# A state kept as diagonal blocks, and a turn of the queries moved behind the second of seven products

## The chip, the cores and the metric

The kernel runs on one core of one Trainium2 chip. Its time is the device time in microseconds (us) of one execution. PE is the matrix engine (PEld its weight loads), DVE the vector engine, ACT the scalar engine, POOL the GpSimd engine and SP the engine whose queue issues the DMAs. Every engine works through its own instructions in the order in which the program lists them, and waits at the first one whose inputs or buffers are not ready.

## The reference

Everything is float32. An RWKV-6 attention block of 4 batches, 8 heads, 768 tokens and a head width of 48 feeds a feed-forward block over 3072 tokens (width 384, inner width 2048):

```python
for t in range(S):
    cur = einsum('bhd,bhe->bhde', u * k[t], v[t])
    y[t] = einsum('bhd,bhde->bhe', r[t], state + cur)
    state = w[t][..., None] * state + einsum('bhd,bhe->bhde', k[t], v[t])
x = y.transpose(0, 2, 1, 3).reshape(B * S, H * D)
h = x @ w_in
out = (h * sigmoid(h)) @ w_out
```

The state of one head is a 48 x 48 matrix. The decay w[t] multiplies its rows.

## The kernel before

**Units.** The work is cut into 12 units, numbered 0 to 11. A unit is 128 tokens of two batches, with all eight heads. Heads stand in pairs on the partitions: the even head of a pair on partitions 0 to 47, the odd one on 64 to 111. In each unit the scan over 128 tokens is done in levels: queries (`tr`) and keys (`tk`) are multiplied by growing products of the decays (`tw`, `tw1` to `tw7`), and for each level PE multiplies keys by queries into scores. `y_state` multiplies the queries by the state, `y_values` the scores by the values, and `update` carries the state over to the next 128 tokens.

**The feed-forward part** of a unit follows one and two units later. `up` (8 steps, L1001) computes `h` and its silu `gt`; then seven products of half matrices, as in a Strassen-Winograd scheme, replace the eight of the plain second multiplication. `quarter(i, which)` (L1053) makes product number `which` of unit i: 16 matmuls of 128 x 192 (L1067) into a tile `p_o`, which has two buffers, and then the additions that use it. They are called q0 to q6 here. q0 is copied by ACT into `partial` (L1074); q1, q2, q3, q5 and q6 are each followed by one addition on DVE (L1076), q4 by two. A product can begin only when the addition of the product two before it has read its buffer. The inputs of three of the seven are differences that `sums` (L1049) makes on DVE.

**The order of the work** is written out by hand. For units 3 to 11 the loop at L1166 takes the lists ("groups") of steps that `mix(i)` returns, and after each group some of the steps of `downs(i - 2) + ups(i - 1)`: these are the seven products of the unit two before, and the eight `up` steps of the unit before. From unit 4 on the numbers of such steps after the groups are `(2, 1, 2, 2, 1, 1, 1, 2, 1, 1, 1)`: q0 and q1 stand behind the first group, q2 behind the second, q3 and q4 behind the third, q5 and q6 behind the fourth. When unit i is spoken of below, its seven products are those issued while `mix(i)` runs, so they belong to the output of unit i - 2.

The steps that the change and the profile below touch:

- `turn(i, b, name)` (L360) transposes the raw rows of one batch with one DVE instruction (L374). "Both" turns are two.
- `grow_own(i, l)` (L649) multiplies keys on POOL, two instructions (L654), and then calls `grow_queries(i, l)`, which multiplies the queries by the decays on DVE in place (L627).
- `start(i)` in `mix` gives the products of the decays for levels 1 to 6 on POOL (L422), and `grow_own(i, 1)`.
- `block_bonus(i, step)` (L505) multiplies parts of r, k and w on POOL (L507) for the scores inside a block of eight tokens. Steps 0 to 3 of a unit are done at the end of the unit before. Step 4 is two instructions that write the tile `ruk`, step 5 is four, and 6 and 7 are one each.
- `block_sum(i, step)` (L539) adds these up on DVE (L541): sum 0 reads the `ruk` of steps 0 and 1, sum 1 what step 2 left in `spare`, sum 2 the `ruk` of step 4 (four instructions). So step 4 on POOL has to wait until sum 0 has read the tile that it overwrites.
- `prepare(i, 3)` and `burst(i, 3)` make the queries of level 3 and the first score matmuls (L704), behind the seven products.
- `move_x(i - 1)` (L921) moves the result y into the layout of the feed-forward part with ten DMAs on SP's queue.
- `update(i, b)` (L885) multiplies the state by the last product of the decays on POOL (L898), and then adds keys times values from PSUM on DVE (L907). For the first 128 tokens it copies instead (L909).

The state of a head pair is kept in a row of 2 x 64 columns: the even head's matrix in columns 0 to 47 of its partitions, the odd head's in columns 64 to 111 of its own. The rest of the row is cleared once (`clear_state`, L403) and never used by a matmul.

Of the kernel before, what the change touches and what calls it, by code (L numbers as in the profile page):

```python
# [8 lines left out]
F32 = mybir.dt.float32  # L9
# [29 lines left out]
def kernel(  # L39
# [11 lines left out]
    nc = tc.nc  # L51

    B, H, S, D = r.shape
    DM, DF = moe_w_in.shape
    L = 128
    NL = 7
    NB = 2
    NP = H // 2
    PD = 64
# [14 lines left out]
    const = ctx.enter_context(tc.tile_pool(name="const", bufs=1))  # L74
# [9 lines left out]
    def bank(name, *dims):  # L84

        have = banks[name][turns_of[name] % 2][:]
        turns_of[name] += 1
        steps, n = [], 1
        for d in dims[::-1]:
            steps.insert(0, [n, d])  # L90
            n *= d
        return bass.AP(tensor=have.tensor, offset=have.offset, ap=[have.ap[0], *steps])
# [193 lines left out]
    make_identity(nc, ident)  # L286


    state = const.tile([128, B, NP, 2 * PD], F32, name="state")

    room = pt.tile([128, 4, DM // 2], F32, name="partial", bufs=1).rearrange("p x d -> p (x d)")
    spread = room[:, 0:4 * L].rearrange("p (s b t) -> p s b t", s=2, b=NB)
# [65 lines left out]
    tw, tr, tk, diag, kq, xt = {}, {}, {}, {}, {}, {}  # L358
# [473 lines left out]
    def values(i, b):  # L832
        return vq[i] if b == 1 else vt[i]

    def y_state(i):

        n, b0 = units[i]
        for e in range(2):
            p_yt[i, e] = bank("p_m", NP, L)
        for p in range(NP):  # L840
            for b in range(NB):
                for e in range(2):
                    rows = slice(PD * e, PD * e + D)
                    nc.tensor.matmul(y_place(i, e, p, b), lhsT=state[rows, b0 + b, p, rows],  # L844
                                     rhs=tr[i][rows, b * NP + p, :], start=(p < 2 and b == 0), stop=False)

        half = L // 2
        for p in range(NP):
            for b in range(NB):
                rows, at = slice(b * half, (b + 1) * half), (2 * p + b) * D  # L850
                nc.tensor.matmul(y_place(i, b, p, b)[:, 0:half], lhsT=whole[i][b][rows, at:at + D],
                                 rhs=score[rows, i % NSC, b, b * NP + p, 0:half], start=False, stop=False)

    def y_place(i, e, p, b):

        x = p % 2
        return p_yt[i, e][PD * x:PD * x + D, p // 2 * NB + b, :]
# [27 lines left out]
    def update(i, b):  # L885
        n, b0 = units[i]
        if n == S // L - 1:
            return
        if b == 0:
            p_kv[i] = bank("p_m" if i < NTOK else "p_sc", NB, NP, D)  # L890
        for p in range(NP):
            for e in range(2):
                nc.tensor.matmul(p_kv[i][PD * e:PD * e + D, b, p, :], lhsT=kq[i, b][:, p, PD * e:PD * e + D],
                                 rhs=values(i, b)[:, 2 * p + e, :], start=(b == 0 and p == 0),
                                 stop=(b == NB - 1 and p == NP - 1))
        new = state[:, b0 + b]
        if n > 0:
            nc.gpsimd.tensor_tensor(out=new, in0=new,  # L898
                                    in1=tw[i][NL][:, b * NP:(b + 1) * NP, :].to_broadcast([128, NP, 2 * PD]),
                                    op=ALU.mult)  # L900
        if b < NB - 1:
            return
        for e in range(2):
            rows, cols = slice(PD * e, PD * e + D), slice(PD * e, PD * e + D)
            new = state[rows, b0:b0 + NB, :, cols]
            if n > 0:
                nc.vector.tensor_tensor(out=new, in0=p_kv[i][rows], in1=new, op=ALU.add)  # L907
            else:
                (nc.scalar.copy if i == 0 else nc.vector.tensor_copy)(out=new, in_=p_kv[i][rows])  # L909
# [23 lines left out]
    def both(fn, i, *args):  # L933
        return [(fn, i, b, *args) for b in range(NB)]

    def block_loads(i, names="wkr"):
        return [(load_blocks, i, name, g) for name in names for g in range(4)]

    def mix(i):

        ahead = i + 1 < len(units)

        def at(now, *steps):
            return steps if now else ()

        def bonus_steps(j, *steps):
            return [(block_bonus, j, x) for x in steps]

        def sum_steps(j, *steps):
            return [(block_sum, j, x) for x in steps]  # L950

        def turns(j):
            return [*both(turn, j, "w"), (product, j, 0), *both(turn, j, "k")]

        def start(j):
            return [*[(product, j, l) for l in range(1, NL)], (grow_own, j, 1)]

        end = [[*at(ahead, *bonus_steps(i + 1, 0, 1, 2, 3))],
               [*at(i < len(units) - NB, (turn_apart, i), (turn_k, i)), (y_state, i), *both(y_values, i), *at(ahead, *turns(i + 1)),
                (sums, i - 1, FH // 2 - 2), *both(update, i), *at(not ahead, (move_x, i))]]  # L960
        if i < NPAIR:
            groups = [[*both(turn, i, "w"), (product, i, 0)],
                      [*both(turn, i, "k"), *both(turn, i, "r"), (odd_ones, i)], [(start_levels, i), (prepare_keys, i, 1)],
                      [(prepare, i, 1), *[(product, i, l) for l in range(1, NL)]],
                      [(burst, i, 1), (keep_level, i, 1)],
                      [(keep_level, i, 2), (go_on, i, 2)],
                      [(prepare, i, 3), (reverse_v, i), (bonus, i, 0)],
                      [(burst, i, 3), (keep_level, i, 3), (bonus_sum, i, 0), (bonus, i, 1), (bonus, i, 2)],
                      [(keep_level, i, 4), (go_on, i, 4), (bonus_sum, i, 1), (load_rk, i + 1), (load_u,)],
                      [(prepare, i, 5), (make_block_mask,), (bonus_spread, i), (bonus_write, i)],  # L970
                      [(burst, i, 5), (keep_level, i, 5), (keep_level, i, 6), (go_on, i, 6)], *end]
        else:
            groups = [[*both(turn, i, "r"), (grow_own, i, 0)], [*start(i), *sum_steps(i, 0, 1), *bonus_steps(i, 4, 5), (move_x, i - 1)],
                      [(odd_keys, i, 2), (grow_keys, i, 2, False), (grow_queries, i, 2), *sum_steps(i, 2)],
                      [(prepare, i, 3), *bonus_steps(i, 6, 7)],
                      [(burst, i, 3), (keep_level, i, 3), *sum_steps(i, 3, 4), (block_move, i), *at(ahead, (load_rk, i + 1))],
                      [(keep_level, i, 4), (go_on, i, 4)],
                      [(prepare, i, 5), (reverse_v, i)],
                      [(block_spread, i), (block_write, i)],
                      [(burst, i, 5), (keep_level, i, 5), (keep_level, i, 6), (go_on, i, 6)], *end]  # L980

        loads = [*at(i >= NPAIR and ahead, *block_loads(i + 1, "r")), *at(i + NSLOT < len(units), *block_loads(i + NSLOT, "wk"))]
        if i + 1 < len(units):
            loads.insert(len(loads) // 2, (load_values, i + 1))

        behind = groups[10 if i < NPAIR else 5 if i == NPAIR else 2:][:4 if i + NSLOT >= len(units) else None]
        for at, group in enumerate(behind):
            group += loads[at * len(loads) // len(behind):(at + 1) * len(loads) // len(behind)]
        return groups
# [127 lines left out]
    for l in range(1, NL):  # L1117
# [9 lines left out]


    others = {1: [(bonus_sum, 1, 0), (bonus_sum, 1, 1), (load_rk, 2), *blocks[8:12]], 2: [*both(update, 0)],
              3: [(bonus_spread, 1), (reverse_v, 1), (clear, 1), (load_values, 2)]}  # L1130

# [4 lines left out]
    for m in range(1, 4):  # L1136
# [4 lines left out]
    do((scores, 1, NL - 1), (bonus, 2, 0), (bonus, 2, 1), (join_weight, 8), (add_weight,), (bonus_sum, 2, 0), (bonus, 2, 2), (up, 0, 7), *both(y, 1), (turn_apart, 1),  # L1141
       (tail_weight, 9), (turn_k, 1), (dense_x, 1, 0), (head_weight, 9, [0]), (dense_x, 1, 1), (head_weight, 9, [1]),
       (join_weight, 9), (add_weight,), (tail_weight, 10), (head_weight, 10), *both(update, 1), (bonus_sum, 2, 1), (load_rk, 3), (up, 1, 0), *both(turn, 2, "w"))
    blocks = block_loads(3)

# [5 lines left out]
    for m in range(6):  # L1151
# [8 lines left out]
    do((burst, 2, 5), (keep_level, 2, 5), (keep_level, 2, 6), (go_on, 2, 6), (bonus_write, 2), (up, 1, 6), (weight_sums, 1),  # L1160
       (load_values, 3), (turn_apart, 2), (turn_k, 2), (up, 1, 7), (weight_sums, 2), (sums, 1, 2))
    do((sums, 1, 3), (y_state, 2), *both(y_values, 2), *both(update, 2),
       (move_x, 2),
       *blocks[7:])

    for i in range(3, len(units)):  # L1166
        steps = downs(i - 2) + ups(i - 1)
        groups = mix(i)
# [40 lines left out]
```

## Time and profile before

| what | value |
|---|---|
| median of 3 runs | 601.27 us (600.91 to 601.62) |
| the profiled execution | 601.18 us, with a span of 599.4 us from first to last instruction |
| granted clock of the matrix engine | 0.999 |
| POOL state multiplication L898 | 16 instructions, 1215 to 2079 ns, median 1266 |
| DVE state addition L907 | 16 instructions, median 551 ns |
| DVE transposes of r, L374 | 20 instructions, median 674 ns |
| DVE additions L1076 | 77 instructions, about 0.35 us each |

The profile comes from the one profiled execution. In its listings a row of a timeline has the start and the length in us, the engine, the line of the kernel, the operation, what it writes and reads with shapes, and how many instructions were merged. In brackets stand the idle time of the engine before it and what ended that idle time. A row of waits has the total, the number and the longest. Matmul ends are modelled, so a PE that is listed as busy is not always at its peak; a stall shows more surely as a later start of the next product.

### The profile page before, as it was taken

To read this page: it belongs to the slowest core of one execution; us is meant where nothing else is said; L and a number is where in the kernel's file an instruction comes from. 1 tells how busy PE (TensorE), PEld (TensorE's weight loads), DVE (VectorE), ACT (ScalarE), POOL (GpSimd) and SP (SyncE) were. 2 spreads that over 40 slices of the span, in tenths; PEclk is the share of its full clock that TensorE was granted. 3 is DMA by queue.
4 is the path that set the end of the run, shared out by engine and by line. 5 is a ranking of instruction groups with operands and counts; after the bars stand their busy time and mean duration, and the time that the engine had idled before them with its cause. 6 is when DMAs were issued, how large, how long until landed. Compare 5 with 4: busy or idle time off the path is not lost.

```text
span 599.4 us, 15465 instructions
## 1 busy us (share of the span) xinstructions
PE 590.6 (99%) x6142; PEld 529.7 (88%) x6142; DVE 417.5 (70%) x709; ACT 232.8 (39%) x516; POOL 361.3 (60%) x414
## 2 busy tenths in 40 slices
PE   8999999999999999999999999999999999999997
PEld 7787876799899899899899889889889889889997
DVE  7879788798696695696696696687588587542041
ACT  6788884431530530540350351361351251250110
POOL 6998778357678568278578478577567567500000
PEclk9999999999999999999999999999999999999999
DMA  9966794342542543642643643643543531101000
GB/s 225 306 143 176 165 277 49 54 80 48 129 61 62 108 68 54 134 63 52 137 63 54 134 61 53 135 61 53 112 77 52 121 57 27 36 2 28 27 1 26
DMA packets 203080, 53.45 MB, mean 89 GB/s; under 512 B 186752, under 2 KB 194816, under 8 KB 203008
## 3 DMA queue, kind: packets, MB, share of 16 engines
q1 hardware_dynamic: 201424, 51.88, 42.3%
q8 instruction: 48, 0.79, 0.6%
q10 hardware_dynamic: 1584, 0.59, 0.5%
q14 instruction: 24, 0.20, 0.1%
HBM read 43.21 MB, written 5.24 MB: 81 GB/s over the span
## 4 chain that ended last, share of the span: by engine, by line
PE 74%; DVE 9%; POOL 4%; DMA 4%; ACT 3%; issue 3%; SPq 3%; DVEq 0%; POOLq 0%; ACTq 0%
PE p_h L1001 31%; PE p_o L1067 31%; PE p_m L1023 3%; PE p_sc L704 2%; PE p_m L865 2%; DVE temps L1049 2%; SPq L123 1%; PE p_m L844 1%; PE p_m L704 1%; DVE score L722 1%; POOL w_in_sb L255 1%; DMA tokens_w<-in_w_dram 1%; POOL tk L645 1%; DVE p_w L242 1%; DMA raw<-in_r_dram 1%
## 5 line engine op out<-in xcount | busy, mean ns | idle before, releaser
L1001 PE MATMUL p_h<-xt,w_in_sb 128*128 128x256 f32 x1152 | 259.5, 382 | 0.8 <-POOL tk L669 0.7
L1001 PEld LDWEIGHTS p_h<-xt,w_in_sb 128*128 128x128 f32 x1152 | 215.6, 190 | 32.1 <-POOL tk L669 0.9
L1010 ACT ACTIVATE gt<-p_h 128x512 f32<-128x512 f32 x90 | 53.5, 596 | 175.4 <-PE p_h L1001 175.1
L645 POOL TENSOR_TENSOR tk<-tk,tw 128x256 f32<-128x256 f32 x128 | 94.6, 759 | 32.9 <-issue 20.8
L1067 PE MATMUL p_o<-own,temps 128*128 128x192 f32 x528 | 88.7, 327 | 0.7 <-DVE temps L1076 0.7
L1067 PEld LDWEIGHTS p_o<-own,temps 128*128 128x128 f32 x528 | 86.0, 190 | 1.6 <-DVE temps L1076 1.6
L507 POOL TENSOR_TENSOR ruk<-tokens_rk 128x768 f32<-128x768 f32 (+1 forms) x32 | 50.6, 1594 | 60.8 <-DMA tokens_rk<-in_k_dram 36.9
L1067 PE MATMUL p_o<-w_out_sb,gt 128*128 128x192 f32 x508 | 86.6, 327 | 0.0
L1067 PEld LDWEIGHTS p_o<-w_out_sb,gt 128*128 128x128 f32 x508 | 83.3, 190 | 1.0 <-DVE partial L1076 0.4
L1049 DVE TENSOR_TENSOR temps<-gt 128x256 f32<-128x256 f32 x84 | 54.9, 653 | 25.5 <-ACT gt L1010 25.3
L627 DVE TENSOR_TENSOR tr<-tr,tw 128x512 f32<-128x512 f32 x61 | 54.8, 899 | 18.3 <-PE p_m L704 14.6
L422 POOL TENSOR_TENSOR tw<-tw 128x256 f32<-128x256 f32 (+6 forms) x83 | 41.0, 494 | 35.8 <-DVE tw L374 31.9
L615 ACT COPY tk<-tk 128x256 f32<-128x256 f32 x52 | 21.0, 403 | 105.2 <-POOL tk L645 77.6
L1049 DVE TENSOR_TENSOR temps<-temps,gt 128x256 f32<-128x256 f32 x43 | 32.6, 759 | 1.5
L722 DVE COPY_PREDICATED score<-mask,p_sc 128x512 f32<-128x512 int8 x42 | 31.2, 799 | 3.5 <-PE p_sc L704 3.3
L1067 PE MATMUL p_o<-w_out_sb,temps 128*128 128x192 f32 x176 | 30.4, 326 | 0.0
L541 DVE TENSOR_REDUCE block_sums<-ruk 128x4 f32<-128x192 f32 (+1 forms) x48 | 24.2, 546 | 7.1 <-POOL ruk L507 7.1
L1067 PEld LDWEIGHTS p_o<-w_out_sb,temps 128*128 128x128 f32 x176 | 28.9, 190 | 0.0
L1076 DVE TENSOR_TENSOR partial<-p_o,partial 128x192 f32<-128x192 f32 x33 | 11.7, 354 | 24.6 <-PE p_o L1067 24.6
L1076 DVE TENSOR_TENSOR temps<-p_o,partial 128x192 f32<-128x192 f32 x22 | 7.9, 358 | 29.8 <-PE p_o L1067 23.5
L870 ACT COPY yt<-p_m 48x512 f32<-48x512 f32 x40 | 23.2, 580 | 13.8 <-PE p_m L865 13.1
L704 PEld LDWEIGHTS p_sc<-tr,tk 48*32 48x32 f32 (+1 forms) x1312 | 18.2, 119 | 11.1 <-issue 8.1
(188 smaller groups left out, 821.9 us busy)
## 6 DMA issues: line engine op xcount, KB each, us to landing
w_out_sb<-in_moe_w_in_dram SPq DMA_DIRECT2D x6, 768.0 KB, 7.5
w_out_sb<-in_moe_w_out_dram SPq DMA_DIRECT2D x4, 768.0 KB, 5.6
own<-in_moe_w_out_dram SPq DMA_DIRECT2D x4, 768.0 KB, 6.4
tokens_rk<-in_r_dram SPq DMA_DIRECT2D x8, 384.0 KB, 4.5
tokens_rk<-in_k_dram SPq DMA_DIRECT2D x8, 384.0 KB, 5.5
tokens_w<-in_w_dram SPq DMA_DIRECT2D x8, 384.0 KB, 6.6
xt<-yt SPq DMA_DIRECT2D x60, 48.0 KB, 2.0
raw<-in_w_dram SPq DMA_DIRECT2D x80, 32.0 KB, 2.0
```

The costliest lines, as they stand in the source:

```text
L422: engine.tensor_tensor(out=up, in0=t[:, :, 0::2], in1=t[:, :, 1::2], op=ALU.mult)
L507: mul = lambda out, one, two: nc.gpsimd.tensor_tensor(out=out, in0=one, in1=two, op=ALU.mult)
L541: add = lambda out, have: nc.vector.tensor_reduce(out=out, in_=have, axis=mybir.AxisListType.X, op=ALU.add)
L627: nc.vector.tensor_tensor(out=odd, in0=odd, in1=tw[i][l][:, :, 0::2][:, :, :, None].to_broadcast([128, Q, L >> (l + 1), c]), op=ALU.mult)
L645: nc.gpsimd.tensor_tensor(out=out, in0=have, in1=odd_products(i, l, b, *blocks), op=ALU.mult)
L704: nc.tensor.matmul(to, lhsT=tk[i][rows, X[l % 2] + p, x * m:(x + 1) * m], rhs=have, start=True, stop=True)
L722: nc.vector.copy_predicated(out=dst, mask=masks[l][:, :, None].to_broadcast([128, NB, NP, ni, c]), data=sc[e].rearrange("p (b q) (i c) -> ...
L870: nc.scalar.copy(out=yt[i][PD * e:PD * e + D, x::2, :, :], in_=p_yt[i, e][PD * x:PD * x + D].rearrange("p (q b) t -> p q b t", b=NB))
L1001: nc.tensor.matmul(p_h[:, a, :], lhsT=w_in_sb[:, c, f * 128:(f + 1) * 128], rhs=xt[i][:, c, :], start=(c == 0), stop=(c == KC - 1))
L1010: nc.scalar.activation(out=gt[i, m], in_=p_h, func=AF.Silu)
L1049: nc.vector.tensor_tensor(out=out, in0=one, in1=two, op=op)
L1067: nc.tensor.matmul(p, lhsT=left(f), rhs=right[:, f, :], start=(f == 0), stop=(f == FH - 1))
```

## The change

The state keeps only the 48 columns that are used: `[128, B, NP, 48]` instead of `[128, B, NP, 128]`. Both heads of a pair then have their matrix in columns 0 to 47, each on its own partitions. `y_state` and `update` address it accordingly, and the POOL multiplication of a batch has 4 x 48 elements to a partition instead of 4 x 128.

In `mix`, for units 4 to 11 (the branch that the diff shows; unit 3 has a list of its own), the first group becomes empty. The turns of r and `grow_own(i, 0)`, which stood ahead of q0 and q1, go to the head of the second group, ahead of `start(i)`. Block sum 1 and block bonus 5 go from the second group to the head of the third, that is behind q2. In the built program PE, ACT, POOL and SP have their instructions in the same order as before. On DVE the addition of q1 now stands ahead of the two turns and the first query step, and the addition of q2 ahead of block sum 1.

```diff
-    state = const.tile([128, B, NP, 2 * PD], F32, name="state")
+    state = const.tile([128, B, NP, D], F32, name="state")
...
-                    nc.tensor.matmul(y_place(i, e, p, b), lhsT=state[rows, b0 + b, p, rows],
+                    nc.tensor.matmul(y_place(i, e, p, b), lhsT=state[rows, b0 + b, p, :],
...
-                                    in1=tw[i][NL][:, b * NP:(b + 1) * NP, :].to_broadcast([128, NP, 2 * PD]),
+                                    in1=tw[i][NL][:, b * NP:(b + 1) * NP, :].to_broadcast([128, NP, D]),
...
-            rows, cols = slice(PD * e, PD * e + D), slice(PD * e, PD * e + D)
-            new = state[rows, b0:b0 + NB, :, cols]
+            rows = slice(PD * e, PD * e + D)
+            new = state[rows, b0:b0 + NB]
...
-            groups = [[*both(turn, i, "r"), (grow_own, i, 0)], [*start(i), *sum_steps(i, 0, 1), *bonus_steps(i, 4, 5), (move_x, i - 1)],
-                      [(odd_keys, i, 2), (grow_keys, i, 2, False), (grow_queries, i, 2), *sum_steps(i, 2)],
+            groups = [[], [*both(turn, i, "r"), (grow_own, i, 0), *start(i), *sum_steps(i, 0), *bonus_steps(i, 4), (move_x, i - 1)],
+                      [*sum_steps(i, 1), *bonus_steps(i, 5), (odd_keys, i, 2), (grow_keys, i, 2, False), (grow_queries, i, 2), *sum_steps(i, 2)],
```

## The prediction

> **What bounds the kernel now.** I read the page's busy times and slices first, then a table of busy time by unit, then the waits of PE, then the timeline of one undisturbed unit.
>
> ```profile
> PE 590.6 (99%) x6142; PEld 529.7 (88%) x6142; DVE 417.5 (70%) x709; ACT 232.8 (39%) x516; POOL 361.3 (60%) x414
> PE   8999999999999999999999999999999999999997
> ```
>
> TensorE is busy from end to end, so a change can win only PE's few stalls, or add some. By unit (start of one unit's seven products to the next; columns: stretch, length, PE busy, ...):
>
> ```profile
> 172.16:219.00 46.84, 46.53 (x498) 42.39 (x497) 35.56 (x59) 15.33 (x38) 33.45 (x38) 1.00 0.42 78
> 219.00:265.00 46.00, 46.00 (x498) 42.37 (x497) 33.38 (x55) 15.34 (x38) 28.71 (x35) 1.00 0.46 83
> 265.00:311.60 46.60, 46.43 (x498) 42.29 (x497) 35.32 (x59) 15.33 (x38) 32.59 (x37) 1.00 0.46 83
> ```
>
> Units 5 and 7 to 9 take exactly 46.00 us: no stall. Units 4 and 6 lose 0.6 to 0.8 us. The waits of the weight loads (total us, times, longest) say where:
>
> ```profile
> PEld p_o L1067 <- DVE temps L1076: 1.6, 3, 0.6
> PEld p_o L1067 <- DVE partial L1076: 0.4, 2, 0.2
> ```
>
> The products q0 to q6 have two PSUM buffers: q3 needs DVE's addition of q1, q5 that of q3. Unit 4, the bad case:
>
> ```profile
> 180.02 0.36 DVE L1076 TENSOR_TENSOR temps<-p_o,partial 128x192 f32<-128x192 f32 x1
> 180.44 5.47 PE L1067 MATMUL p_o<-own,temps 128*128 128x192 f32 x32 [0.31 <-DVE temps L1076]
> ```
>
> q3 could have started 7.80 after q0 (172.16), at 179.96; it starts 0.48 late, 0.41 after the addition began, and the restart costs 0.11 more (5.47 for a stretch of 5.36). Then q5 is held too: addition 185.42, start 185.82. Together 0.77 (19.06 from q0 to the next score matmuls, against 18.29 in unit 8); the same reading gives 0.63 in unit 6 and 0.57 in unit 3. **1.96 us of stall**, all because q1's addition is queued on DVE behind the turns of r. Now unit 8, undisturbed, DVE, POOL and PE:
>
> ```profile
> 360.95 1.29 DVE L374 STREAM_TRANSPOSE tr<-raw 128x512 f32<-128x512 f32 x2
> 362.27 1.05 DVE L627 TENSOR_TENSOR tr<-tr,tw 128x512 f32<-128x512 f32 x1
> 363.36 0.36 DVE L1076 TENSOR_TENSOR temps<-p_o,partial 128x192 f32<-128x192 f32 x1
> 363.63 0.68 DVE L627 TENSOR_TENSOR tr<-tr,tw 128x512 f32<-128x512 f32 x1
> 364.23 0.95 DVE L541 TENSOR_REDUCE block_sums<-ruk 128x16 f32<-128x768 f32 x1
> ...
> 367.71 1.13 DVE L541 TENSOR_REDUCE block_sums<-ruk 128x4 f32<-128x192 f32 x4 [0.89 <-POOL ruk L507]
> 368.76 0.35 DVE L1076 TENSOR_TENSOR partial<-p_o,partial 128x192 f32<-128x192 f32 x1
> ```
>
> ```profile
> 361.34 1.44 POOL L654 TENSOR_TENSOR tk<-tk,tw 128x256 f32<-128x256 f32 x2
> 365.26 2.42 POOL L507 TENSOR_TENSOR ruk<-tokens_rk 128x384 f32<-128x384 f32 x2 [2.48 <-DVE block_sums L541]
> ```
>
> ```profile
> 357.56 5.36 PE L1067 MATMUL p_o<-w_out_sb,gt 128*128 128x192 f32 x32
> 362.76 7.96 PE L1067 MATMUL p_o<-own,temps 128*128 128x192 f32 x48
> 370.56 2.76 PE L1067 MATMUL p_o<-w_out_sb,gt 128*128 128x192 f32 x16
> ```
>
> See a chain that crosses engines: block sum 0 (364.23) lets POOL multiply into ruk (365.26), that lets block sum 2 start (367.71), and behind it on DVE stands q3's addition (368.76), which q5 (370.56) needs. It has 1.4 us to spare now, because the turns start 2.0 us before q1 is done.
>
> **What the Trainium skill says.** "SBUF — State Buffer", section Who interferes with whom: a VectorE operation with two SBUF inputs contends with a GpSimd one that reads SBUF; with one SBUF input, or as a tensor_reduce, it does not. The trace agrees: the first query step (L627, both inputs in SBUF) takes 1.05 us overlapping POOL's L654, 0.76 in unit 11 with a shorter overlap, and 0.68 at 12.34 us with POOL idle; the additions L1076 (one input in PSUM) take 0.35 to 0.36 everywhere. "Perfetto Trace Analysis", Optimizing Tensor Performance, Matmuls: matmul groups should rotate through PSUM banks so that evacuation overlaps; here two buffers do, until the addition is late.
>
> **The change, part by part.**
>
> State width. The decay of the state on POOL shrinks from 512 to 192 elements:
>
> ```profile
> L898 POOL TENSOR_TENSOR state<-state,tw x16: 1215/1266/2079, 121.8 to 448.0; 128x512 f32<-128x512 f32 x16
> ```
>
> The nearest row, POOL L507 with 128x192, takes 0.59. So 16 x (1.27 - 0.59) = 11 us of POOL go; but POOL then waits for DVE (2.48 us before L507), so its own saving is hidden by PE. It frees DVE of contention: in units 2 to 3 a difference (L1049) at 124.13 takes 1.25 instead of 0.42 beside L898. The 0.83 us won there is more than the 0.57 - 0.11 = 0.46 that unit 3's q1 addition is late, so unit 3's stall goes (bounds: 0 to 0.57 gained; I take 0.57). DVE's L907 and the two copies L909 write as many elements as before (48x384), and y_state loads the same 48 columns, now at another offset: 0, bounded by 0.1 us for 16 additions off the path. The clear (1.81 us at 9.30, now about 0.7) is hidden: POOL waits 2.66 us for DVE after it.
>
> The move. A turn is two transposes on DVE; grow_own is two POOL products (L654) and one DVE query step; start adds the small POOL products, two more L654 and a query step; block sum 1 is one DVE reduction, block_bonus 5 four POOL operations. No DMA moves: the ten of move_x and the block loads keep their places on SP's queue. PE, ACT and POOL keep their order too. On DVE just two things change places: q1's addition goes ahead of the turns and the first query step, and q2's ahead of sum 1. So q1's addition is never late again: the stalls of units 4 and 6 (1.40) go as well. **Gain 1.96 us.**
>
> The price: q1's addition waits for PE, and the turns, both query steps and sum 0 now wait behind it, with POOL's ruk product, sum 2 and q3's addition behind those. Unit 11 shows when an addition of q1 that really waits begins: 499.68, with q0 at 494.21 (544.33 and 538.87 after the last unit): 5.46 after q0. From there, start to start: addition to turns 0.28 (363.36 to 363.63); turns to first query step 1.32; that step 0.68 plus 0.04 to a dependent one (POOL's L654 ended at 362.78, 5.2 after q0, and ends earlier now, so no contention at 7.06): 0.72; second query step to sum 0 0.60; sum 0 to sum 2 through POOL 3.48 (364.23 to 367.71; the same DVE work lies beside it, so I keep it); sum 2 to q3's addition 1.05. Sum: 5.46 + 7.45 = 12.91 after q0. q5 can start 0.40 later, at 13.31; it would start at 13.00. Late by 0.31, plus 0.11 for the restart: **0.42 us in each of the eight units 4 to 11, 3.36 us.** Bounds: with q3's addition at 12.5 nothing is lost; with a first query step of 1.05 and its gap the stall is 0.79. q4's start needs q2's addition, at 5.46 + 2.92 + 0.87 = 9.25, free at 9.65 against 10.4: covered. POOL's keys for the next scores end 1.65 later, at 17.2 after q0; PE wants them at 18.7: covered by q6. If that cover shrank, the scores would be next.
>
> Sum: 601.18 - 1.96 + 3.36 = 602.6 for the profiled execution, which lies 0.09 below the median 601.27, so 602.7. A difference of 0.2% (1.2 us) is about what can be told from none.
>
> **Rivals.**
> - No new stall (faster). If q3's addition starts before 12.5 after q0, 0.4 earlier than worked out, q5 never waits and only the gain is left: 601.27 - 1.96 = 599.3. For it: q3's addition has 1.4 us of slack now. Against: the 2.0 us delay of the turns is larger than slack plus what the contention gives back (0.37) and q1's addition, no longer inside the chain (0.28). Chance 0.08.
> - A draw: 0.1 to 0.28 us per unit, 8 x 0.2 = 1.6 against 1.96: 600.9 (600.1 to 601.5). It needs the chain 0.15 to 0.3 shorter. Chance 0.15.
> - A longer chain: the first query step stays at 1.05, or the eight DMA semaphores that the turn waits on are worked off only after q1's addition. 0.79 per unit, 6.3 - 2.0: 605.6. Against: in unit 8 turns follow sums without a gap. Chance 0.15.
> - The likeliest: 0.42 per unit, 602.7, own range 601.6 to 604.0. Chance 0.62.
>
> **How the numbers follow.** Slower by over 0.2% (above 602.5): the longer chain 0.15 and some 0.45 of the likeliest; within 0.2%: the draw and the rest of the likeliest, 0.32; faster: 0.08. The range runs from inside the draw to short of the longer chain's full price: 600.6 to 605.3.
>
> **What would show it.** Right: units 5 and 7 to 9 go from 46.00 to 46.4 us; PEld waits at L1067 name "DVE partial L1076", eight times about 0.4, and "DVE temps L1076" is gone; DVE waits for PE before q1's addition; first query step 0.68; L898 near 0.6. Wrong: units still at 46.00, a first query step of 1.05, or the wait at q4 or at the scores (L704).

## The result and the profile after

| | before | after |
|---|---|---|
| median, both in the same session | 601.44 us (600.54 to 601.66, 6 runs) | 604.44 us (603.88 to 606.19, 6 runs) |
| profiled execution | 601.18 us, span 599.4 | 603.92 us, span 602.1 |
| ratio after to before | | 1.0053, 95% interval 1.0042 to 1.0064 |

The changed kernel is 0.5% slower. The loss comes in nearly equal portions, one in each of the eight units 4 to 11. The table of busy time by unit for the changed kernel (stretch from q0 to the next q0, length, then busy time of PE, PEld, DVE, ACT and POOL, clock, DMA share, GB/s) shows it for units 5 to 8:

```profile
218.30:264.87 46.57, 46.27 (x498) 42.34 (x497) 32.30 (x54) 15.32 (x38) 28.28 (x35) 1.00 0.46 84
264.87:311.43 46.56, 46.26 (x497) 42.34 (x496) 33.98 (x60) 15.33 (x38) 31.52 (x37) 1.00 0.46 82
311.43:358.00 46.57, 46.27 (x497) 42.34 (x496) 32.30 (x57) 15.33 (x38) 30.94 (x36) 1.00 0.45 82
358.00:404.57 46.57, 46.27 (x498) 42.34 (x497) 33.91 (x57) 15.32 (x38) 31.09 (x37) 1.00 0.45 80
```

Before, the quiet units took 46.00 and the two bad ones 46.77 (unit 4) and 46.63 (unit 6). Now every unit from 5 to 10 takes 0.56 or 0.57 more than its quiet length. I measured all units between the starts of q0's copy on ACT. The losses of units 4 to 11 are 0.49, 0.57, 0.56, 0.57, 0.57, 0.56, 0.56 and 0.64, in sum 4.52 us. Against them stand the old stalls of units 4 and 6, 0.77 and 0.63, and 0.48 by which unit 3 is shorter. With 0.13 lost ahead of unit 3's first copy, 4.52 - 1.88 + 0.13 = 2.77, and the profiled executions differ by 2.74.

The waits of PE and of its weight loads name one cause (waiting engine, buffer and line, what it waited for, then total us, times, longest):

```profile
PEld p_o L1067 <- DVE partial L1076: 4.7, 8, 0.7
PE p_o L1067 <- DVE partial L1076: 2.4, 8, 0.4
```

That is one wait in each of eight units for an addition that writes `partial`. The row "DVE temps L1076" is gone from both engines. Unit 8 shows which addition it is. DVE's timeline of the changed kernel:

```profile
363.46 0.36 DVE L1076 TENSOR_TENSOR temps<-p_o,partial 128x192 f32<-128x192 f32 x1 [2.85 <-ACT tk L615]
363.86 1.31 DVE L374 STREAM_TRANSPOSE tr<-raw 128x512 f32<-128x512 f32 x2
365.20 1.42 DVE L627 TENSOR_TENSOR tr<-tr,tw 128x512 f32<-128x512 f32 x2
366.53 0.95 DVE L541 TENSOR_REDUCE block_sums<-ruk 128x16 f32<-128x768 f32 x1
367.39 0.35 DVE L1076 TENSOR_TENSOR partial<-p_o,partial 128x192 f32<-128x192 f32 x1
...
370.01 1.13 DVE L541 TENSOR_REDUCE block_sums<-ruk 128x4 f32<-128x192 f32 x4 [0.90 <-POOL ruk L507]
371.06 0.61 DVE L1076 TENSOR_TENSOR partial<-p_o,partial 128x192 f32<-128x192 f32 x2
```

The two rows of POOL that lie in the chain, and PE's first six products (q0 and q1 in the first row, q2 to q4 in the second, q5 in the third):

```profile
360.92 1.44 POOL L654 TENSOR_TENSOR tk<-tk,tw 128x256 f32<-128x256 f32 x2
367.56 2.42 POOL L507 TENSOR_TENSOR ruk<-tokens_rk 128x384 f32<-128x384 f32 x2 [5.21 <-DVE block_sums L541]
```

```profile
358.00 5.36 PE L1067 MATMUL p_o<-w_out_sb,gt 128*128 128x192 f32 x32
363.20 7.96 PE L1067 MATMUL p_o<-own,temps 128*128 128x192 f32 x48
371.46 2.87 PE L1067 MATMUL p_o<-w_out_sb,gt 128*128 128x192 f32 x16 [0.30 <-DVE partial L1076]
```

Read them in this order. DVE sits idle for 2.85 us ahead of q1's addition (363.46). That wait is put down to ACT, whose copy was over at 362.79; what came last is PE's q1, which ended at about 363.36. Only then come the turns, the query steps and sum 0. POOL stands still for 5.21 us until sum 0 has read `ruk`, where it stood still for 2.48 before. Sum 2 follows POOL, and q3's addition at last starts at 371.06, 13.06 after q0. Before, it started 11.20 after q0. PE's q5 starts 0.40 later, at 13.46, where 13.00 was its undisturbed time, and its 16 matmuls take 2.87 instead of 2.76.

The narrower state did what the arithmetic said, with a slightly larger duration. POOL's decay in the changed kernel (minimum, median and maximum in ns):

```profile
L898 POOL TENSOR_TENSOR state<-state,tw x16: 677/732/1547, 122.0 to 449.2; 128x192 f32<-128x192 f32 x16
```

And DVE in unit 3, where the two differences took 1.15 and 1.25 beside it before:

```profile
123.19 0.61 DVE L1049 TENSOR_TENSOR temps<-temps,gt 128x256 f32<-128x256 f32 x1
123.73 0.72 DVE L1049 TENSOR_TENSOR temps<-gt 128x256 f32<-128x256 f32 x1
...
131.01 0.36 DVE L1076 TENSOR_TENSOR temps<-p_o,partial 128x192 f32<-128x192 f32 x1
```

q1's addition of unit 3 comes 6.78 after q0 (124.23) instead of 7.84, and PE no longer waits for it.

### The profile page after: what moved, and what is told of

It reads as the page before. It is cut to its first block, busy times and chain, and to the rows that moved or that the text cites. A ratio compares the mean times of both kernels' runs of the same rounds, so it can differ in the third digit from the quotient of the medians.

```text
span 602.1 us, 15464 instructions
## 1 busy us (share of the span) xinstructions
PE 592.0 (98%) x6142; PEld 530.0 (88%) x6142; DVE 409.7 (68%) x709; ACT 232.7 (39%) x516; POOL 351.8 (58%) x414
## 4 chain that ended last, share of the span: by engine, by line
PE 44%; SPq 17%; DVE 11%; POOL 9%; DMA 9%; issue 5%; ACT 3%; DVEq 0%; POOLq 0%; ACTq 0%
PE p_h L1001 17%; PE p_o L1067 17%; SPq L123 13%; DMA tokens_w<-in_w_dram 5%; POOL ruk L507 3%; DVE block_sums L541 3%; PE p_m L1023 3%; DVE tr L627 3%; POOL tk L645 3%; SPq L143 2%; PE p_sc L704 2%; DMA raw<-in_k_dram 2%; DVE tr L374 2%; DVE score L722 2%; POOL w_in_sb L255 1%
## 5 line engine op out<-in xcount | busy, mean ns | idle before, releaser
L645 POOL TENSOR_TENSOR tk<-tk,tw 128x256 f32<-128x256 f32 x128 | 93.8, 754 | 27.8 <-issue 14.4
L507 POOL TENSOR_TENSOR ruk<-tokens_rk 128x768 f32<-128x768 f32 (+1 forms) x32 | 50.4, 1586 | 76.6 <-DMA tokens_rk<-in_k_dram 38.3
L1067 PE MATMUL p_o<-w_out_sb,gt 128*128 128x192 f32 x508 | 87.2, 328 | 2.4 <-DVE partial L1076 2.4
L1067 PE MATMUL p_o<-own,temps 128*128 128x192 f32 x528 | 87.9, 326 | 0.0
L1067 PEld LDWEIGHTS p_o<-w_out_sb,gt 128*128 128x128 f32 x508 | 83.0, 190 | 5.3 <-DVE partial L1076 4.7
L1067 PEld LDWEIGHTS p_o<-own,temps 128*128 128x128 f32 x528 | 86.1, 190 | 0.1
L1049 DVE TENSOR_TENSOR temps<-gt 128x256 f32<-128x256 f32 x84 | 50.3, 598 | 26.9 <-ACT gt L1010 26.8
L627 DVE TENSOR_TENSOR tr<-tr,tw 128x512 f32<-128x512 f32 x61 | 55.3, 906 | 16.7 <-PE p_m L704 12.6
L1076 DVE TENSOR_TENSOR temps<-p_o,partial 128x192 f32<-128x192 f32 x22 | 7.9, 358 | 47.9 <-PE p_o L1067 22.9
L1067 PE MATMUL p_o<-w_out_sb,temps 128*128 128x192 f32 x176 | 30.4, 326 | 0.0
L1067 PEld LDWEIGHTS p_o<-w_out_sb,temps 128*128 128x128 f32 x176 | 28.9, 190 | 0.0
L654 POOL TENSOR_TENSOR tk<-tk,tw 128x256 f32<-128x256 f32 x32 | 27.6, 882 | 0.0
L1049 DVE TENSOR_TENSOR temps<-temps,gt 128x256 f32<-128x256 f32 x43 | 26.3, 612 | 1.5
```

The source lines that it names most:

```text
L507: mul = lambda out, one, two: nc.gpsimd.tensor_tensor(out=out, in0=one, in1=two, op=ALU.mult)
L627: nc.vector.tensor_tensor(out=odd, in0=odd, in1=tw[i][l][:, :, 0::2][:, :, :, None].to_broadcast([128, Q, L >> (l + 1), c]), op=ALU.mult)
L645: nc.gpsimd.tensor_tensor(out=out, in0=have, in1=odd_products(i, l, b, *blocks), op=ALU.mult)
L1049: nc.vector.tensor_tensor(out=out, in0=one, in1=two, op=op)
L1067: nc.tensor.matmul(p, lhsT=left(f), rhs=right[:, f, :], start=(f == 0), stop=(f == FH - 1))
```

## The experiments

The theory: q5 waits for q3's addition, which stands at the end of a chain that now begins with q1's addition. Its rivals: the loss comes from the narrow state, from the displaced sum 1, or from contention between DVE and POOL. "Diff" is against the changed kernel unless said otherwise, and each ratio is to the kernel before in the same session.

**The two parts apart.** First the narrow state with the old order of steps:

```diff
-            groups = [[], [*both(turn, i, "r"), (grow_own, i, 0), *start(i), *sum_steps(i, 0), *bonus_steps(i, 4), (move_x, i - 1)],
-                      [*sum_steps(i, 1), *bonus_steps(i, 5), (odd_keys, i, 2), (grow_keys, i, 2, False), (grow_queries, i, 2), *sum_steps(i, 2)],
+            groups = [[*both(turn, i, "r"), (grow_own, i, 0)], [*start(i), *sum_steps(i, 0, 1), *bonus_steps(i, 4, 5), (move_x, i - 1)],
+                      [(odd_keys, i, 2), (grow_keys, i, 2, False), (grow_queries, i, 2), *sum_steps(i, 2)],
```

> The narrow state with the order of before. Theory (the loss is the wait of q5 for the addition of q3, which the new order made late; narrowing only takes POOL off DVE's shared reads): no q5 wait, unit 3's stall gone, and DVE some 0.8 us earlier in units 4 and 6, so that their stalls of 0.77 and 0.63 go as well or shrink below 0.2: 599.3 to 600.2, ratio to before 0.997 to 0.998, units of 46.0 us. Rival (the narrow layout itself costs, through PE's state matmuls or POOL): slower than before, 603 to 605, with longer y_state matmuls or L898 on the path.

Measured: 599.80 against 601.64 us, 0.9978 (0.9967 to 0.9989). No wait at L1067 is left. Units 4 to 9 take 46.00, of which unit 8 by the table of busy time:

```profile
356.42:402.42 46.00, 46.00 (x498) 42.37 (x497) 32.26 (x57) 15.32 (x38) 30.86 (x36) 1.00 0.45 82
```

PE is busy for all of it. So the narrow state alone takes away the stalls of units 3, 4 and 6, although the turns still stand ahead of q1's addition. Unit 4 says why: its two differences took 1.15 and 1.26 before and take 0.61 and 0.72 here, so everything behind them on DVE comes about 1.1 us sooner. (Unit 3 as a whole is only 0.10 shorter, 47.86 against 47.96, though its wait at L1067 is gone. That unit varies from 47.3 to 48.6 in the profiles; more on this below, with the small copy.)

Next the new order alone, with the state kept at 2 x 64 columns (the old lines of `state`, `y_state` and `update` put back):

> The new order with the wide state. Theory: eight waits at q5 of about 0.56 us each (4.5 in all), units 4 and 6 lose their old stalls (1.40), unit 3 keeps its 0.57: 601.4 - 1.4 + 4.5 = 604.5, ratio 1.005, slightly slower than the whole change. Rival (the narrow layout costs, the order gains): 600.0, ratio 0.998.

Measured: 604.69 against 601.64, 1.0049 (1.0037 to 1.0061). Units 5 to 9 take 46.56 or 46.57, as with the whole change. The waits of PE:

```profile
PE p_o L1067 <- DVE partial L1076: 2.4, 8, 0.4
PE p_o L1067 <- DVE temps L1076: 0.2, 1, 0.2
```

The eight new waits are all there, and of the three old ones only unit 3's, whose list the order doesn't touch. The new order carries the loss. It also removes the stalls of units 4 and 6, so these could be removed by either part.

**The two moves of the order apart.** Only sum 1 and bonus 5 behind q2, the turns at their old place:

```diff
-            groups = [[], [*both(turn, i, "r"), (grow_own, i, 0), *start(i), *sum_steps(i, 0), *bonus_steps(i, 4), (move_x, i - 1)],
+            groups = [[*both(turn, i, "r"), (grow_own, i, 0)], [*start(i), *sum_steps(i, 0), *bonus_steps(i, 4), (move_x, i - 1)],
```

> Narrow state, the turns of r in front of q0 as before, and only block sum 1 and block bonus 5 moved behind q2. Theory (moving the turns is what makes q3's addition late): no wait at q5, like the narrow state alone: 599.8, ratio 0.997 to 0.998. Rival (moving sum 1 and bonus 5 delays q3's addition or the keys): waits at L1067 or L704, 602 to 604.

Measured: 600.42 against 601.75, 0.9981 (0.9967 to 0.9994), and no wait at L1067. Moving sum 1 costs nothing that the products show. The profiled execution took 601.77, because unit 5 took 47.74; there PE waited for the transfers of `move_x`:

```profile
PE p_h L1001 <- DMA xt<-yt: 1.5, 1, 1.5
```

Now the turns alone moved, sum 1 and bonus 5 in the second group as before:

```diff
-            groups = [[], [*both(turn, i, "r"), (grow_own, i, 0), *start(i), *sum_steps(i, 0), *bonus_steps(i, 4), (move_x, i - 1)],
-                      [*sum_steps(i, 1), *bonus_steps(i, 5), (odd_keys, i, 2), (grow_keys, i, 2, False), (grow_queries, i, 2), *sum_steps(i, 2)],
+            groups = [[], [*both(turn, i, "r"), (grow_own, i, 0), *start(i), *sum_steps(i, 0, 1), *bonus_steps(i, 4, 5), (move_x, i - 1)],
+                      [(odd_keys, i, 2), (grow_keys, i, 2, False), (grow_queries, i, 2), *sum_steps(i, 2)],
```

> Narrow state, the turns and the first query step moved behind q1 as in the change, but block sum 1 and block bonus 5 left in the second group, ahead of q2's addition. Theory: q2's addition 0.46 later than in the change, at about 9.85 after q0, free for q4 at 10.25 where q4 begins at 10.40: just covered; q3's addition as in the change (13.06), wait at q5 about 0.56: 604.4, ratio 1.005. Rival (sum 1 behind q2 is part of the price): 602 or less. Second rival (q2's addition is no longer covered): a wait at q4 too, 605 or more.

Measured: 604.59 against 601.75, 1.0040 (1.0028 to 1.0053), units of 46.56 to 46.57 again. DVE's timeline of unit 8, with q0 at 358.66:

```profile
368.06 0.54 DVE L541 TENSOR_REDUCE block_sums<-spare 128x8 f32<-128x384 f32 x1
368.51 0.35 DVE L1076 TENSOR_TENSOR partial<-p_o,partial 128x192 f32<-128x192 f32 x1
```

q2's addition now stands behind sum 1, at 9.85 after q0 instead of 9.39. Its cover holds (q4 can start 0.40 later, at 10.25, and wants to at 10.40). q5 starts at 372.12, again 13.46 after q0, because DVE waits for POOL's `ruk` in any case. The whole loss is the move of the turns. Nor is it new contention: between the additions of q1 and q3 one DVE step runs beside POOL's `ruk` products, and it takes 0.99 in the changed kernel (at 368.12) and 0.98 before (at 365.83).

**Cutting the chain at its end.** Sum 2 goes behind q4's two additions, so q3's addition no longer waits for POOL:

```diff
-                      [*sum_steps(i, 1), *bonus_steps(i, 5), (odd_keys, i, 2), (grow_keys, i, 2, False), (grow_queries, i, 2), *sum_steps(i, 2)],
-                      [(prepare, i, 3), *bonus_steps(i, 6, 7)],
+                      [*sum_steps(i, 1), *bonus_steps(i, 5), (odd_keys, i, 2), (grow_keys, i, 2, False), (grow_queries, i, 2)],
+                      [*sum_steps(i, 2), (prepare, i, 3), *bonus_steps(i, 6, 7)],
```

> The whole change, but block sum 2 goes behind the additions of q3 and q4 on DVE. Theory: the addition of q3 no longer stands behind POOL's product, it begins about 10.6 us after q0 (when PE is done with q3), q5 starts 13.0 after q0, no wait of PE at L1067 is left: units of 46.0 us and about 599.5, ratio 0.997. Rival (the later queries or keys hold the score matmuls, or sum 2 and POOL's last block products become late in turn): PE waits at L704 instead, 602 or more.

Measured: 599.91 against 601.64, 0.9970 (0.9961 to 0.9979). DVE's timeline of unit 8 (q0 at 356.14), then PE's:

```profile
367.18 0.34 DVE L1076 TENSOR_TENSOR partial<-p_o,partial 128x192 f32<-128x192 f32 x1
...
369.88 1.12 DVE L541 TENSOR_REDUCE block_sums<-ruk 128x4 f32<-128x192 f32 x4
```

```profile
356.14 5.36 PE L1067 MATMUL p_o<-w_out_sb,gt 128*128 128x192 f32 x32
361.34 7.96 PE L1067 MATMUL p_o<-own,temps 128*128 128x192 f32 x48
369.14 2.76 PE L1067 MATMUL p_o<-w_out_sb,gt 128*128 128x192 f32 x16
```

Turns, query steps and sum 0 are as late as in the changed kernel (sum 0 at 8.53 after q0 in both). Only q3's addition is earlier, at 11.04 after q0, and q5 starts at 13.00 without a wait. So it is the end of the chain, and not the late turns as such, that costs the time. The same kernel in a later session, beside the last experiment below:

> The whole change with block sum 2 behind the additions of q3 and q4 again, beside the next version, on one chip. Theory: no wait at L1067, units of 46.00 us, ratio to before 0.997; in some executions PE waits for the last of move_x's ten DMAs in unit 5, where SP issues it at 237.1 and PE's first up matmul stands at 237.5: its times spread upward from 599.2.

Measured: 601.01 against 602.01, 0.9983 (0.9969 to 0.9996), again with units of 46.00, unit 5 excepted with 46.18.

**Shortening the chain in the middle.** Sum 0 goes ahead of the turns, so POOL gets `ruk` sooner:

```diff
-            groups = [[], [*both(turn, i, "r"), (grow_own, i, 0), *start(i), *sum_steps(i, 0), *bonus_steps(i, 4), (move_x, i - 1)],
+            groups = [[], [*sum_steps(i, 0), *both(turn, i, "r"), (grow_own, i, 0), *start(i), *bonus_steps(i, 4), (move_x, i - 1)],
```

> The whole change, but block sum 0 stands ahead of the turns of r, right behind the addition of q1: the same DVE work between the additions of q1 and q3, but POOL's 2.4 us of ruk products run beside the turns. Theory (the chain through POOL sets it): addition of q3 at 12.3 to 12.9 us after q0 instead of 13.06; the first query step now contends with POOL and takes about 1.05; wait at q5 0 to 0.2 us per unit: 599.5 to 601.2. Rival (the amount of DVE work between the two additions sets it, POOL's product fits beside it): q3's addition stays at 13.0 to 13.1, 604.

Measured: 602.43 against 601.64, 1.0014 (1.0006 to 1.0022). This missed: a gain was expected. DVE's timeline of unit 8 (q0 at 357.99), and the wait that came instead:

```profile
365.91 2.36 DVE L627 TENSOR_TENSOR tr<-tr,tw 128x512 f32<-128x512 f32 x2
368.19 0.34 DVE L1076 TENSOR_TENSOR partial<-p_o,partial 128x192 f32<-128x192 f32 x1
...
370.78 0.34 DVE L1076 TENSOR_TENSOR partial<-p_o,partial 128x192 f32<-128x192 f32 x1
```

```profile
PEld p_o L1067 <- DVE partial L1076: 2.6, 8, 0.3
```

q3's addition came at 12.79, early enough for q5. But POOL's `ruk` products (364.75 to 366.73) and the one after them now run beside the two query steps, which take 2.36 us instead of 1.42. That is the contention of two SBUF readers which the Trainium skill describes in "SBUF — State Buffer", section Who interferes with whom: an operation of DVE with two SBUF inputs contends with one of POOL that reads SBUF. The trace agrees, and gives the size: 0.94 us for the two. The profiles together say more: the one that starts second pays. A query step that begins while POOL is inside a product takes what is left of that product plus 0.55 us (at least 0.68), and one that begins first takes about 0.68, whatever POOL begins beside it. This fits all 854 query steps (L627) of the 14 profiled executions within 0.03 us. The step of 1.05 us in the kernel before is one: it began at 362.27, and POOL's product ended at 362.78. In the other direction, POOL's products of 128x192 (L507) take 0.58 to 0.61 us, and 0.91 to 1.10 where a DVE operation with two SBUF inputs was already running.

q2's addition slips to 10.20 after q0, so q4 starts at about 10.60 instead of 10.40, plus 0.11 for the restart: 0.31, and PE's row of q2, q3 and q4 reads 8.27 instead of 7.96. The wait moved from q5 to q4.

To see whether that q4 wait is the only one left, the second query step goes behind q2's addition as well (a function `own_keys` takes the POOL part of `grow_own`):

```diff
+            groups = [[], [*sum_steps(i, 0), *both(turn, i, "r"), (grow_own, i, 0), *start(i)[:-1], (own_keys, i, 1), *bonus_steps(i, 4), (move_x, i - 1)],
+                      [(grow_queries, i, 1), *sum_steps(i, 1), *bonus_steps(i, 5), (odd_keys, i, 2), (grow_keys, i, 2, False), (grow_queries, i, 2), *sum_steps(i, 2)],
```

> Sum 0 ahead of the turns as in the earlier run, and the second query step moved behind q2's addition, POOL's order unchanged. Theory (between the additions of q1 and q3 DVE has more work, with the contention of the query steps, than the 7.1 us that PE leaves): q2's addition at about 9.2 after q0, no wait at q4; but q3's addition stays near 12.8 and the wait moves back to q5, about 0.3 us per unit: 602.0, no better than with the wait at q4. Rival (the wait at q4 was the only one left): no wait, 599.7.

Measured: 600.86 against 601.75, 0.9984 (0.9963 to 1.0005). No wait at L1067, and units of 46.00 except unit 5. DVE in unit 8, with q0 at 361.56 (L1080 is L1076 of the other listings):

```profile
369.48 1.35 DVE L627 TENSOR_TENSOR tr<-tr,tw 128x512 f32<-128x512 f32 x1
370.76 0.34 DVE L1080 TENSOR_TENSOR partial<-p_o,partial 128x192 f32<-128x192 f32 x1
371.02 0.81 DVE L627 TENSOR_TENSOR tr<-tr,tw 128x512 f32<-128x512 f32 x1
...
373.86 0.34 DVE L1080 TENSOR_TENSOR partial<-p_o,partial 128x192 f32<-128x192 f32 x1
```

My own theory had put the wait back at q5, and was wrong. q3's addition came at 12.30: the later query step began when only 0.27 us of a POOL product was left (0.81 in all), and the one after it just ahead of the next product (0.68, against 0.90 in the run before). The rival, that the q4 wait was the only one, held. The profiled execution took 605.17: its unit 5 lost 4.26 us. PE waited 2.3 of them for `xt` as above, until 242.16, and from 242.90 on its granted clock was halved for 3.4 us (stretch, length, PE busy, clock, DMA share, GB/s):

```profile
242.90:246.30 3.40, 3.40 (x10) 0.50 0.63 161
```

By that share the lower clock cost some 1.7 (an estimate), so the wait and the clock are nearly all of the 4.26. From 246.30 on the clock was 1.00 again. After the wait of 1.5 us with sum 1 alone moved it stayed at 1.00. That the longer wait brought the lower clock with it fits the order in time, but is not shown.

**The semaphores ahead of the turns.** Each turn needs rows that DMAs bring. A tiny DVE copy that reads the same rows, put into the empty first group, makes DVE work off those waits while it waits for PE anyway:

```diff
+    touched = const.tile([128, 4], F32, name="touched")
+
+    def touch(i):
+        room = raw[:, i % NSLOT, WRK["r"]].rearrange("p b h d -> p (b h d)").rearrange("p (q g d) -> p q g d", q=Q, d=32)
+        nc.vector.tensor_copy(out=touched, in_=room[:, 0, :, 0])
...
-            groups = [[], [*both(turn, i, "r"), (grow_own, i, 0), *start(i), *sum_steps(i, 0), *bonus_steps(i, 4), (move_x, i - 1)],
+            groups = [[(touch, i)], [*both(turn, i, "r"), (grow_own, i, 0), *start(i), *sum_steps(i, 0), *bonus_steps(i, 4), (move_x, i - 1)],
```

> The whole change, and one small DVE copy (four elements of each partition of the raw r) in the empty first group, ahead of the addition of q1, so that the eight DMA waits of the first turn are met there. Theory (the 0.12 us by which the changed kernel's step from q1's addition to the turns, 0.40, is longer than the 0.28 that I had used is these waits, worked off behind the addition): the step is 0.28 again, q5 waits 0.44 instead of 0.56 per unit, 1.0 us less than the whole change: 603.4. Rival (the 0.12 belongs to an addition that waited for PE, or to the transposes): step 0.40, time as the whole change, 604.4.

Measured: 604.87 against 601.75, 1.0047 (1.0031 to 1.0064), so no gain in the time. Units 5 to 9 did get shorter, 46.43 to 46.44 instead of 46.57, but unit 3 took 48.63 in the profiled execution (47.48 in the changed kernel). Of that, 0.92 is a wait of PE's first layer for ACT's silu at 158.92, some 20 us ahead of the first copy (179.54). So the copy did not cause it. Whether the other executions lost time in the same place isn't on record, and I ran the kernel again beside the changed kernel itself.

> The whole change again, beside the version with the small copy, on one chip. Both theories: 46.57 us per unit, ratio to before 1.004 to 1.006.

Measured for the changed kernel: 604.72 against 601.96, 1.0041 (1.0025 to 1.0058).

> The whole change with the small DVE copy ahead of q1's addition again. Theory (the eight DMA waits cost 0.12 us per unit, and the missing gain of the first measurement lay in stages before unit 4 that the copy does not touch): 46.43 us per unit, and 1.0 us less than the whole change beside it, ratio to before about 1.003. Rival (the copy costs elsewhere what it wins at q5): the same time as the whole change within 0.4 us.

Measured with the copy: 603.70 against the same 601.96, 1.0029 (1.0020 to 1.0038), so 1.0 us below the changed kernel of the session, though the two intervals overlap. The trace settles the mechanism. DVE in unit 8, then PE's q5 (here L943 is the copy, L1082 is L1076 and L1073 is L1067):

```profile
360.82 0.17 DVE L943 COPY touched<-raw 128x4 f32<-128x4 f32 x1
363.76 0.36 DVE L1082 TENSOR_TENSOR temps<-p_o,partial 128x192 f32<-128x192 f32 x1 [2.76 <-PE p_o L1073]
364.04 1.29 DVE L374 STREAM_TRANSPOSE tr<-raw 128x512 f32<-128x512 f32 x2
```

```profile
371.62 1.57 PE L1073 MATMUL p_o<-w_out_sb,gt 128*128 128x192 f32 x8 [0.17 <-DVE partial L1082]
```

From the addition to the turns it is 0.28 instead of 0.40, and q5 starts at 13.33 after q0 (358.29) instead of 13.46. That is 0.13 in each unit, 8 x 0.13 = 1.0 us. The copy ran at 360.82, so the rows for the turns lay there 3 us before the turns began: DVE does not let them pass the addition that waits for PE.

The waits themselves are in the traces, as instructions of DVE's sequencer (DVEq, the part that waits ahead of the engine), with their number, durations in ns, and first and last start. First the changed kernel, then the kernel before:

```profile
L374 DVEq EVENT_SEMAPHORE  x4: 21/50/50, 363.5 to 363.8; - x4
L374 DVEq EVENT_SEMAPHORE  x4: 21/50/50, 360.3 to 360.5; - x4
```

In the changed kernel they stand between the addition (363.46) and the turns (363.86). Before, they ran beside a difference that was still being made (360.14 to 360.65), and cost nothing.

**Towards something faster.** To the kernel with sum 2 behind q4, one edit that was meant to issue the block loads sooner, so that `move_x` is not late in unit 5:

```diff
-        behind = groups[10 if i < NPAIR else 5 if i == NPAIR else 2:][:4 if i + NSLOT >= len(units) else None]
+        behind = groups[10 if i < NPAIR else 5 if i == NPAIR else 2:][:4 if i + NSLOT >= len(units) else None if i <= NPAIR else -1]
```

> As the version beside it, and for units 5 to 9 the loads of later r, w, k and v are spread over one group fewer, so that none stands behind the last group and fewer loads are ahead of move_x on SP's queue. Theory (the spread of the faster versions comes from x arriving late): move_x is issued several us earlier in unit 5, the median falls by 0.3 to 0.8 us against the version beside it and its times spread less: 599.2. Rival (x is late for another reason, or the loads collide with the block loads): same or slower.

Measured: 600.47 against 602.01, 0.9965 (0.9953 to 0.9978). The time is 0.5 us below the same kernel without the edit, but the intervals overlap, and the edit did little of what it was for: `move_x` of unit 5 was issued 11.89 us after q0 (231.55, q0 at 219.66) against 12.61 (230.78, q0 at 218.17), 0.7 us sooner where several were expected. Other kernels here lie between 11.6 and 13.5 without such an edit. Nothing follows from it. Whether an earlier `move_x` would help was not tried in another way.

So several versions beat both kernels, by 0.2 to 0.4% of the time before: the narrow state with the old order (599.80), the same with sum 1 behind q2 (600.42), and the new order with sum 2 behind q4 (599.91, repeated 601.01, and 600.47 with the last edit). Which of them is fastest these runs don't tell.

## Why the prediction was right, and where its sum was short

**The mechanism** held: the bound (PE, with a stall only where a PSUM buffer comes free late), the size of the gain, the new wait at q5, and the path to it through POOL. The size of the loss held less well. 602.7 was forecast and 604.44 measured. That is inside the whole range, but above the 601.6 to 604.0 that was given for the likeliest case, and the median rose by 3.00 where about 1.4 was forecast. The range took it in because it reached towards the longer chain, and half of that rival, the semaphores, came true.

**The term that was mis-sized** is the stall per unit: 0.42 forecast, 0.565 on average measured, and 8 x 0.145 = 1.16 of the 1.34 us by which the profiled execution's +1.4 fell short of +2.74. Most of the rest is the 0.13 lost ahead of unit 3 and a gain of 1.88 instead of 1.96. The parts of the chain, in unit 8:

| step, start to start | forecast | measured |
|---|---|---|
| q0 to q1's addition | 5.46 | 5.46 |
| addition to turns | 0.28 | 0.40 |
| turns to first query step | 1.32 | 1.34 |
| first query step to sum 0 (0.72 + 0.60) | 1.32 | 1.33 |
| sum 0 to sum 2, through POOL | 3.48 | 3.48 |
| sum 2 to q3's addition | 1.05 | 1.05 |
| q3's addition to q5 | 0.40 | 0.40 |
| sum | 13.31 | 13.46 |

The step that failed is "addition to turns 0.28 (363.36 to 363.63)". It was read between an addition and a query step, whose inputs were on DVE already; the turn has DMA waits of its own. The rival "a longer chain" named them, and the copy ahead of the addition showed them: 0.12 us a unit. The rival's reason against, that "in unit 8 turns follow sums without a gap", was the misreading: those waits ran while the engine still had work to finish, and show only behind an instruction that itself had to wait. The rival's other half, a first query step of 1.05, did not come: the two steps take 1.42 together, free of POOL.

One sum in the rivals doesn't hold as written. Against "no new stall" it sets a delay of the turns of 2.0 us, "larger than" 1.4 + 0.37 + 0.28. Those add up to 2.05. The delay that belongs there is from 3.39 after q0 to 5.46 + 0.28 = 5.74, so 2.35 (2.47 measured: 363.86 less 358.00, less 3.39). With it the conclusion stands, and it did come true; the main sum of the chain doesn't use the 2.0. Two smaller figures are off by a little: q3's addition is early enough up to 12.60 (13.00 - 0.40), not 12.5, and the keys come 1.71 later by its own chain, not 1.65.

**The gain** of 1.96 was right in size: 1.88 by the units, and the narrow state alone brought 1.84 of the median. Its split was not. The prediction gave 1.40 to the move and 0.57 to the narrow state; the first two experiments show that the narrow state removes all three stalls and the order two of them. The price would therefore have been paid for nothing even had it been small. The prediction looked at the stretched differences of unit 3 only, though the kernel before has the same two in front of unit 4's q1 addition (1.15 us at 171.47, 1.26 us at 172.54).

**The smaller points.** L898 came to 0.73 where "near 0.6" was taken from a product without a broadcast operand. Unit 3's addition came 1.06 us sooner, 0.83 was forecast, since both differences got shorter. q2's addition started at 9.39 (forecast 9.25) and POOL's keys ended at 17.3 (17.2); both covers held. The waits were eight, named as forecast, though "about 0.4" was too low for the weight loads (4.7 / 8 = 0.59).

"No new stall" is ruled out by the eight waits, and the draw, which needed 0.1 to 0.28 us in a unit, by the 0.57. Moving one sum behind q4 turns the change into "no new stall".

## What to carry to other kernels

On an engine that works in order, an instruction that waits for another engine delays everything behind it, so ask of every step that is put behind it which chain it begins, and follow that chain across engines to the next buffer that PE needs. When a late release is the trouble, look for the step that stands directly ahead of the releasing instruction and waits for a third engine: here moving that one (sum 2) took the wait away at once, while shortening the chain in its middle moved the wait to q4 and needed a second move. Before paying for a reordering, see whether another part of the same change has already removed the stall that it is for.

## What was not expected of the hardware

- A DVE instruction that needs rows from several DMAs starts 0.40 us after the one ahead of it, not 0.28, when that one had itself waited for PE. A copy of four elements to a partition, which waits for them earlier, takes 0.17 us and brings the step back to 0.28.
- The same two query steps take 1.42 us with POOL idle and 2.36 us beside its products, so bringing POOL's work forward slowed DVE's by 0.94 us. What decides is which of the two starts first: the second waits for what is left of the other's operation.
- After PE had waited 2.3 us for `xt` in one execution, its granted clock fell to 0.50 for 3.4 us, which cost about 1.7 us more.
- With the stall at q5 gone, unit 5 shows the next thin cover: PE's first layer waited for the transfers of `move_x` for 1.5 and 2.3 us in two profiled executions (sum 1 alone moved, and sum 0 first with the later query step) and for 0.2 in a third; the other profiles list no such wait. In all three the last of the ten DMAs was issued late, 18.5 to 19.2 us after q0 (17.3 to 18.4 in the others), and in the first two it also landed only 3.4 and 3.5 us after its issue, where 2.0 is usual. Why is open.
